# A planned kernel on one core: layer 1's activation and tails worked in PSUM, GpSimd's passes cut into 256 columns

## The chip, the core and the metric

The kernel runs on one core of a Trainium2 chip. The metric is the device time of one execution in microseconds (us), from launch to the last output; lower is better. The engines are named as in the profile: PE (TensorE's matmuls), PEld (its weight loads), DVE (VectorE), ACT (ScalarE), POOL (GpSimd) and SP (SyncE, which here only issues DMAs).

## What is computed

The first part is an attention with positive random features, for 8 batches of 8 heads, 576 positions, 64 dimensions and 128 features. The second is a two-layer network on its output, 4608 tokens of 512 features, with 2048 hidden ones; its weights come as float64.

```python
def phi(x):
    proj = einsum('bhsd,md->bhsm', x, omega)
    h = proj - sum(x * x, -1) / 2
    h = h - max(h, -1)
    return exp(h) / sqrt(m)
q_p, k_p = phi(q * scale), phi(k * scale)
num = q_p @ (k_p^T v);  den = q_p . sum(k_p) + 1e-06
x = (num / den), laid out as 4608 tokens x 512
h = x @ w_in
g = where(h > 0, h, exp(min(h, 0)) - 1)
out = g @ w_out
```

## The kernel before

The work is split twice. Attention goes by pairs of heads, 32 of them (8 batches with 4 pairs each). The network goes by 12 blocks of 384 tokens, and each block by 16 steps of 128 hidden features, 192 steps in all. The first three blocks run their steps 0 to 7 first and 8 to 15 later, so that the weights of the second half may be converted later (SPLIT, line 65).

A step has two layers. `layer1` (line 936) makes 12 matmuls into a bank of PSUM with the tag "ph", of which there are two. Numbers are kept as a high and a low part in fp32r, so each product takes three matmuls. Then ACT takes relu(-h) (L958) and exp(-that) (L959) into an SBUF tile e, DVE makes max(e - 1, h) out of e and the bank (L962), again in e. The high half g[0] is a cast of e (L967, by ACT or DVE, shown as L355 or L357 of the helper `copy`), and the low half g[1] is e minus that (L969, by POOL or DVE, shown as L360 of the helper `tt`). `layer2` (line 974) makes 9 matmuls of 512 columns into three banks acc0 to acc2, which a block keeps over its steps.

A pair is loaded (`load_pair`), its k and q are projected (`project`), k's features are summed against v (`kv`), and `finish` divides q's features by the denominator. The first 7 pairs of k and 8 of q are projected from their native layout ("native", L461), the others with fp32r parts ("tk", "tq", L512). The division has four slots of 128 columns at a time, on POOL as a rule (L706, shown as L360 hq). The first pairs, NEARLY of them, take their PSUM from the banks acc0 to acc2 and ph; later ones from three banks "pa" (`bank`, line 392).

`from_f64` (line 848) turns 512 columns of float64 weights into high and low fp32r halves: ACT L874 and L878, DVE L882, L889 and L894, POOL L897 (an integer sum, 512 columns), a cast to the high half and a subtraction for the low half on POOL (512 columns). This is done for each of the 16 slices of both weight matrices; slices of w1 are also stored in DRAM (w1s) and read again for the later blocks (w1c).

The order on each engine is not written by hand. Each operation is given to `Plan.op` with the engines that may run it, a duration in ns, a due time in us, and what it reads and writes. `Plan.order` (line 149) simulates: on each free engine the ready operation with the lowest due goes next, a bank or buffer is given in turn, and DVE operations marked `port=True` do not start in it while a POOL operation runs, nor the other way round. The result is a fixed order for each engine's queue; at run time semaphores hold it. All due times are worked out from a few numbers at the top: MLP0 is the due of the first step, SEG and STEP are the spacing of steps, LAG how far layer 2 is behind layer 1, DUE_* and *2 how far the parts of a pair lie ahead of its end, CONV* the same for the weights. ALT gives for a kind of operation by how many us the second engine is held back from taking it (negative: preferred).

```python
op("ACT", act(TB, True), due, lambda: nc.scalar.activation(e(), ph(), AF.Relu, scale=-1.0), (p,), (e,))
op("ACT", act(TB), due + 0.2, lambda: nc.scalar.activation(e(), e(), AF.Exp, scale=-1.0), (e,), (e,))
op("DVE", dve(TB), due + 0.8,
   lambda: nc.vector.scalar_tensor_tensor(e(), e(), -1.0, ph(), ALU.add, ALU.max), (p, e), (e,))
```

Of the kernel before, what the change touches and what calls it, by code (L numbers as in the profile page):

```python
# [9 lines left out]
F32 = mybir.dt.float32  # L10
# [30 lines left out]
NNAT = dict(k=7, q=8)  # L41


MLP0 = 58
SEG = [8.62, 5.76, 4.29, 5.37, 3.5, 5.86]
STEP = 4.9
STEP_ATT = 6.59

LAG = 3.08


PAIR0 = 9.46
# [12 lines left out]
SPLIT = (0, 8, 16)
NHALF = 3

DUE_Z = 12.84

NEARLY = 4  # L70

NSWAP = 8

# [198 lines left out]

ALT = dict(kv=1, out=-0.1, conv_clamp=-1, conv_hi=-1, conv_sub=2, g_hi=0, g_lo=1, y_hi=None, y_lo=-0.38, norm=2, turn=2, x_hi=0.55, sq=0.19)


def other(kind, *engs):
    return () if ALT[kind] is None else [(eng, ns, ALT[kind]) for eng, ns in zip(engs[::2], engs[1::2])]


def mm(n, m=1):

    return m * (n / 2.4 + 2.5)
# [15 lines left out]
def performer_elu_kernel(  # L300
# [58 lines left out]
    def tt(e, *args):  # L359
        (nc.vector if e == "DVE" else nc.gpsimd).tensor_tensor(*args)  # L360
# [294 lines left out]
    def finish(i, due):  # L655
# [26 lines left out]
        for g in range(3):  # L682
            d = due - 9 + g
            js = slice(4 * g, min(4 * g + 4, NJ))
            n = js.stop - js.start
            slots = [(j, j % 2, slice(0, P)) for j in range(4 * g, 4 * g + 4)]
            if g == 2:
                slots = [(8, a, slice(a * D, a * D + D)) for a in range(2)]
            hg = (h, g) if native(i, "q") else (h, min(g, 1))

            def dens(slots=slots):
                for j, a, r in slots:
                    junk = Buf(sb, [P, M], F32, "junk", f"junk_{i}_{j}_{a}", 2)
# [10 lines left out]
            op(
                "POOL", 145 + 214 * n, d + 1.2,
                lambda e, js=js, n=n: tt(  # L706
                    e, h()[:, js], h()[:, js], den()[:, js].unsqueeze(2).to_broadcast([P, n, M]), ALU.mult
                ),
                (hg, (den, g)), ((h, "n", g),), alt=other("norm", "DVE", dve(n * M)), port=True,
            )  # L710
            if i >= NTURN:
                blocks(i, g, h, qt, due - 5 + g)
                continue
            p = bank(i, "pa", f"pt_{i}_{g}")

            def turn(g=g, p=p, js=js):
                for e, j in enumerate(range(js.start, js.stop)):
                    nc.tensor.transpose(p()[:, e * P:(e + 1) * P], h()[:, j, :], ident)

            def src(g=g, p=p):  # L720
                if g == 2:
                    return p()[:, 0:P].rearrange("p (a x) -> p a x", a=2)
                return p().rearrange("p (t a x) -> p a t x", t=2, a=2)

            def dst(x, g=g):
                if g == 2:
                    return x[:, :, 512:S]
                return x[:, :, g * 256:(g + 1) * 256].rearrange("p a (t x) -> p a t x", t=2)

            d = due - 5 + g  # L730
            op("PE", 109 * n, d, turn, ((h, "n", g),), (p,))
            op(
                "ACT", act(n * P, True), d + 0.5, lambda e, src=src, dst=dst: copy(e, dst(qh()), src()), (p,), ((qh, g),),
                alt=other("turn", "DVE", dve(n * P)),
            )
# [31 lines left out]
    def blocks(i, g, h, qt, due):  # L767

        n = 4 if g < 2 else 1
        js = slice(4 * g, 4 * g + n)  # L770

        def turn():
            for o in range(2 if g == 2 else 1):
                nc.vector.transpose(
                    qt()[:, js.start + o:js.stop + o].rearrange("p j x -> p (j x)"),
                    h()[:, js].rearrange("p j x -> p (j x)"),
                )

        op("DVE", (1 if g < 2 else 2) * dve(n * P), due, turn, ((h, "n", g),), ((qt, g),))

    def output(i, qt, due):

# [65 lines left out]
    def from_f64(src, hi, lo, nm, due, key):  # L848
# [13 lines left out]
        def low():  # L862
            return words()[:, :, 0]
# [4 lines left out]
        def ui():  # L868
            return u().bitcast(I32)
# [24 lines left out]
            lambda: nc.vector.scalar_tensor_tensor(ui(), up(), -(2 ** 31), ui(), ALU.bitwise_and, ALU.bitwise_or),  # L894
            (u, (raw, 1)), (u,), port=True,
        )
        op("POOL", pool(512), due - 5, lambda: nc.gpsimd.tensor_tensor(ui(), ui(), low(), ALU.add), (u, (raw, 0)), (u,))  # L897
        op(
            "ACT", act(512), due - 4, lambda e: copy(e, hi(), u()), (u,), (key + ("h",),),
            alt=other("conv_hi", "DVE", dve(512, True)), port=True,  # L900
        )
        op(
            "POOL", pool(512), due - 3,
            lambda e: tt(e, lo(), u(), hi().bitcast(F32), ALU.subtract), (u, key + ("h",)), (key + ("l",),),
            alt=other("conv_sub", "DVE", dve(512)), port=True,
        )

    w1c, gt, acc = {}, {}, {}

    def weights(F, due):  # L910
# [4 lines left out]
        def flat():  # L915
            return t().rearrange("p a c -> p (a c)").bitcast(F32)

        both = ((t, "h"), (t, "l"))
        if blk == 0:
            from_f64(w1[f], lambda: t()[:, 0], lambda: t()[:, 1], f"w1_{f}", due, (t,))  # L920
            op("SP", 500, due, lambda: nc.sync.dma_start(w1s[f], flat()), both, (("w1s", f),), P * 4096)
# [14 lines left out]
    def layer1(F, due):  # L936
# [15 lines left out]

        for c in range(NC):
            reads = [(z, k) for k in ring(blk) if k[1] == c for z in ("xh", "xl")]
            op("PE", mm(TB, 3), due + 0.5 * c, lambda c=c: mms(c), [*reads, (w, "h"), (w, "l")], (p,))
        due += 2

        op("ACT", act(TB, True), due, lambda: nc.scalar.activation(e(), ph(), AF.Relu, scale=-1.0), (p,), (e,))  # L958
        op("ACT", act(TB), due + 0.2, lambda: nc.scalar.activation(e(), e(), AF.Exp, scale=-1.0), (e,), (e,))  # L959
        op(  # L960
            "DVE", dve(TB), due + 0.8,
            lambda: nc.vector.scalar_tensor_tensor(e(), e(), -1.0, ph(), ALU.add, ALU.max), (p, e), (e,),  # L962
        )
        first, second = ("ACT", act(TB)), ("DVE", dve(TB, True))
        if blk:
            first, second = second, first
        op(*first, due + 1.2, lambda x: copy(x, g()[:, 0], e()), (e,), ((g, 0),), alt=other("g_hi", *second), port=True)  # L967
        op(
            "POOL", pool(TB), due + 1.5,  # L969
            lambda x: tt(x, g()[:, 1], e(), g()[:, 0].bitcast(F32), ALU.subtract), (e, (g, 0)), ((g, 1),),  # L970
            alt=other("g_lo", "DVE", dve(TB)), port=True,
        )

    def layer2(F, due):
        blk, f, f0, f1 = STEPS[F]
        g = gt.pop(F)
        for tt in range(NTT):
# [157 lines left out]
```

## Time and profile before

| | us |
|---|---|
| median of 3 runs | 1058.7 (1058.46 to 1059.76) |
| the profiled execution | 1058.12 |
| its span, first to last instruction | 1056.3 |
| busy: PE, ACT, DVE, POOL | 1024.7, 725.9, 674.9, 488.1 |

The profiled execution is the one that every row below comes from. Its span leaves out 1.8 us around the instructions. Matmuls are pipelined, so two that follow each other overlap in the rows and PE's busy time is a union. The granted TensorE clock was 0.992 of full speed in the mean.

### The profile page before, as it was taken

How to read it: one execution, taken by the hardware profiler on the slowest of the kernel's cores; microseconds unless marked ns; L12 is line 12 of the kernel's file. 1: busy time of each engine (PE TensorE's matmuls, PEld its weight loads, DVE VectorE, ACT ScalarE, POOL GpSimd, SP SyncE). 2: the span in 40 equal slices, each digit the busy share in tenths (PEclk: the TensorE clock that was granted, in tenths of full speed). 3: DMA queues.
4: the chain of work that ended last, by engine and by line, in shares of the span. 5: the costliest groups of instructions: out<-in, count | busy, mean ns of one | idle time of the engine just before them, and what ended most of it. 6: DMA issues, size and time to landing. Idle time of an engine off the chain costs nothing.

```text
span 1056.3 us, 22323 instructions
## 1 busy us (share of the span) xinstructions
PE 1024.7 (97%) x7171; PEld 903.2 (86%) x7171; DVE 674.9 (64%) x2626; ACT 725.9 (69%) x2154; POOL 488.1 (46%) x504
## 2 busy tenths in 40 slices
PE   7987989999999999999999999999999999999998
PEld 6776778789988888898888888998888888899997
DVE  5899888694688877324778787424777786422222
ACT  6987875584888996328999998327999898322221
POOL 1675645565465455224465555323544664322221
PEclk8999999999999999999999999999999999999999
DMA  6655667566764755444755556434665553444431
GB/s 199 175 179 157 196 233 240 190 227 238 228 214 136 232 187 171 151 137 133 238 168 187 181 185 211 153 120 139 202 191 180 190 182 97 143 138 137 150 121 69
DMA packets 70533, 185.00 MB, mean 175 GB/s; under 512 B 7952, under 2 KB 23504, under 8 KB 70416
## 3 DMA queue, kind: packets, MB, share of 16 engines
q1 hardware_dynamic: 70416, 183.57, 53.3%
q8 instruction: 58, 0.95, 0.4%
q14 instruction: 59, 0.48, 0.1%
HBM read 161.78 MB, written 21.76 MB: 174 GB/s over the span
## 4 chain that ended last, share of the span: by engine, by line
PE 77%; ACT 1%; DMA 1%; issue 1%; DVE 0%; POOL 0%; SPq 0%; POOLq 0%; DVEq 0%
PE ph L949 11%; PE acc L983 11%; PE acc L985 11%; PE ph L951 11%; PE acc L984 11%; PE ph L950 11%; PE pn L795 3%; PE pkv L573 3%; PE ppq L512 3%; PE ppk L512 2%; DMA w1c<-w1s 1%; PE pz L672 1%; DMA xk<-in_kx_dram 0%; ACT hk L428 0%; PE pkv L583 0%
## 5 line engine op out<-in xcount | busy, mean ns | idle before, releaser
L360 POOL TENSOR_TENSOR g<-e,g 128x384 fp32r<-128x384 f32 x174 | 190.6, 1095 | 392.6 <-DVE g L357 321.4
L949 PE MATMUL ph<-xh,w1c 128*128 128x384 f32 x768 | 264.1, 344 | 3.2 <-DVE e L962 1.6
L951 PE MATMUL ph<-xh,w1c 128*128 128x384 f32 x768 | 258.9, 337 | 0.0
L950 PE MATMUL ph<-xl,w1c 128*128 128x384 f32 x768 | 258.3, 336 | 0.0
L962 DVE SCALAR_TENSOR_TENSOR e<-e,ph 128x384 f32<-128x384 f32 x192 | 105.8, 551 | 218.1 <-ACT e L959 213.0
L958 ACT ACTIVATE e<-ph 128x384 f32<-128x384 f32 x192 | 94.1, 490 | 205.7 <-PE ph L951 204.1
L983 PE MATMUL acc<-w2h,g 128*128 128x512 f32 x576 | 230.3, 400 | 0.1
L985 PE MATMUL acc<-w2h,g 128*128 128x512 f32 x576 | 228.1, 396 | 1.2 <-DVE g L360 1.1
L984 PE MATMUL acc<-w2l,g 128*128 128x512 f32 x576 | 227.9, 396 | 0.0
L949 PEld LDWEIGHTS ph<-xh,w1c 128*128 128x128 f32 x768 | 144.6, 188 | 21.4 <-issue 6.0
L950 PEld LDWEIGHTS ph<-xl,w1c 128*128 128x128 f32 x768 | 144.7, 188 | 9.8
L951 PEld LDWEIGHTS ph<-xh,w1c 128*128 128x128 f32 x768 | 144.3, 188 | 0.0
L985 PEld LDWEIGHTS acc<-w2h,g 128*128 128x128 f32 x576 | 108.3, 188 | 27.6 <-DVE g L360 2.0
L983 PEld LDWEIGHTS acc<-w2h,g 128*128 128x128 f32 x576 | 108.3, 188 | 13.9 <-issue 2.1
L984 PEld LDWEIGHTS acc<-w2l,g 128*128 128x128 f32 x576 | 108.4, 188 | 8.9
L959 ACT ACTIVATE e<-e 128x384 f32<-128x384 f32 x192 | 101.2, 527 | 3.4
L360 POOL TENSOR_TENSOR hq<-hq,den 128x512 f32<-128x512 f32 (+1 forms) x96 | 82.4, 873 | 19.7 <-DVE den L703 18.1
L694 DVE CUSTOM_DVE_ANT_0 junk<-hq,pz 128x128 f32<-128x128 f32 (+1 forms) x320 | 73.8, 280 | 9.9 <-PE pz L672 8.8
L530 DVE CUSTOM_DVE_ANT_0 hk<-ppk,p2k 128x128 f32<-128x128 f32 x225 | 56.7, 287 | 29.1 <-ACT p2k L521 27.6
L521 ACT ACTIVATE p2k<-ppk,sqk 128x128 f32<-128x128 f32 x225 | 68.1, 368 | 6.0 <-PE ppk L512 5.1
L521 ACT ACTIVATE p2q<-ppq,sqq 128x128 f32<-128x128 f32 x216 | 66.8, 366 | 7.6 <-PE ppq L512 4.6
L428 ACT ACTIVATE hk<-hk,nbk 128x128 f32<-128x128 f32 x225 | 71.4, 399 | 0.5
(105 smaller groups left out, 1641.5 us busy)
## 6 DMA issues: line engine op xcount, KB each, us to landing
w1c<-w1s SPq DMA_DIRECT2D x176, 512.0 KB, 3.4
raw_w<-in_w_dram SPq DMA_DIRECT2D x32, 512.0 KB, 4.7
xk<-in_kx_dram SPq DMA_DIRECT2D x25, 576.0 KB, 3.8
xq<-in_qx_dram SPq DMA_DIRECT2D x24, 576.0 KB, 4.7
v<-in_v_dram SPq DMA_DIRECT2D x32, 325.0 KB, 3.2
out_dram<-o SPq DMA_DIRECT2D x36, 256.0 KB, 2.5
w1s<-w1c SPq DMA_DIRECT2D x16, 512.0 KB, 4.2
zk<-kvd SPq DMA_DIRECT2D x96, 64.0 KB, 2.7
```

Of the source, the lines that this page charges most:

```text
L360: (nc.vector if e == "DVE" else nc.gpsimd).tensor_tensor(*args)
L521: nc.scalar.activation(p2()[:, a], view()[:, a, M:], AF.Identity, bias=sq()[:, j:j + 1], scale=-1.0)
L694: nc.vector.tensor_tensor_reduce(out=junk()[r], in0=h()[r, j, :], in1=pz()[r, a * P:(a + 1) * P], scale=1.0, scalar=EPS, op0=ALU.mult, op1 ...
L949: nc.tensor.matmul(ph(), wh, xh[:, c, o:o + TB], start=(c == 0), stop=False)
L950: nc.tensor.matmul(ph(), wh, xl[:, c, o:o + TB], start=False, stop=False)
L951: nc.tensor.matmul(ph(), wl, xh[:, c, o:o + TB], start=False, stop=(c == NC - 1))
L958: op("ACT", act(TB, True), due, lambda: nc.scalar.activation(e(), ph(), AF.Relu, scale=-1.0), (p,), (e,))
L959: op("ACT", act(TB), due + 0.2, lambda: nc.scalar.activation(e(), e(), AF.Exp, scale=-1.0), (e,), (e,))
L962: lambda: nc.vector.scalar_tensor_tensor(e(), e(), -1.0, ph(), ALU.add, ALU.max), (p, e), (e,),
L983: nc.tensor.matmul(a(), g()[:, 0, ts], w2h[:, f], start=(f == f0), stop=False)
L984: nc.tensor.matmul(a(), g()[:, 0, ts], w2l[:, f], start=False, stop=False)
L985: nc.tensor.matmul(a(), g()[:, 1, ts], w2h[:, f], start=False, stop=(f == f1 - 1))
```

## The change

Layer 1: L962 writes its result back into the bank ph instead of e. The cast to g[0] and the subtraction for g[1] read ph, and the subtraction is always DVE's. In `from_f64` POOL's sum and its subtraction become two instructions of 256 columns each, and in `finish` the division by the denominator becomes two instructions of two slots. What reads those results now waits for both. NEARLY goes from 4 to 6, and the numbers of due times and preferences are others.

```diff
-MLP0 = 58
-SEG = [8.62, 5.76, 4.29, 5.37, 3.5, 5.86]
-STEP = 4.9
+MLP0 = 116.09
+SEG = [7.76, 5.18, 3.52, 6.03, 3.08, 6.08]
+STEP = 5.77
-LAG = 3.08
-PAIR0 = 9.46
-DUE_LOAD, DUE_K, DUE_KV, DUE_Q = 27.64, 25.53, 12.92, 18.02
-LOAD2, K2, KV2, Q2 = 56.0, 46.17, 29.33, 32.74
-TAIL = 11.71
-TAIL2 = 4.06
+LAG = 3.07
+PAIR0 = 6.93
+DUE_LOAD, DUE_K, DUE_KV, DUE_Q = 13.33, 24.73, 12.92, 16.61
+LOAD2, K2, KV2, Q2 = 61.91, 48.81, 29.33, 33.34
+TAIL = 12.08
+TAIL2 = 3.52
-CONV1 = 13.71
-CONV_STEP = -0.51
-CONV2 = 0.84
-CONV3 = 70.47
+CONV1 = 15.65
+CONV_STEP = -0.39
+CONV2 = 0.86
+CONV3 = 64.8
-DUE_Z = 12.84
-NEARLY = 4
+DUE_Z = 12.4
+NEARLY = 6
-ALT = dict(kv=1, out=-0.1, conv_clamp=-1, conv_hi=-1, conv_sub=2, g_hi=0, g_lo=1, y_hi=None, y_lo=-0.38, norm=2, turn=2, x_hi=0.55, sq=0.19)
+ALT = dict(kv=1.9, out=-5.74, conv_clamp=1.29, conv_hi=9.8, conv_sub=2.06, g_hi=0.02, g_lo=5.17, y_hi=None, y_lo=2.7, norm=0.24, turn=1.44, x_hi=-0.5, sq=-0.57)
...
-            op(
-                "POOL", 145 + 214 * n, d + 1.2,
...
+            for x in range((n + 1) // 2):
+                jx = slice(js.start + 2 * x, min(js.start + 2 * x + 2, js.stop))
+                nx = jx.stop - jx.start
+                op(
+                    "POOL", 145 + 214 * nx, d + 1.2,
+                    lambda e, jx=jx, nx=nx: tt(
+                        e, h()[:, jx], h()[:, jx], den()[:, jx].unsqueeze(2).to_broadcast([P, nx, M]), ALU.mult
+                    ),
+                    (hg, (den, g)), ((h, "n", g, x),), alt=other("norm", "DVE", dve(nx * M)), port=True,
+                )
...
-        op("POOL", pool(512), due - 5, lambda: nc.gpsimd.tensor_tensor(ui(), ui(), low(), ALU.add), (u, (raw, 0)), (u,))
+        for x in range(2):
+            cs = slice(256 * x, 256 * x + 256)
+            op(
+                "POOL", pool(256), due - 5,
+                lambda cs=cs: nc.gpsimd.tensor_tensor(ui()[:, cs], ui()[:, cs], low()[:, cs], ALU.add),
+                (u, (raw, 0)), ((u, x),),
+            )
...
-        op(
-            "POOL", pool(512), due - 3,
-            lambda e: tt(e, lo(), u(), hi().bitcast(F32), ALU.subtract), (u, key + ("h",)), (key + ("l",),),
+        for x in range(2):
+            cs = slice(256 * x, 256 * x + 256)
+            op(
+                "POOL", pool(256), due - 3,
+                lambda e, cs=cs: tt(e, lo()[:, cs], u()[:, cs], hi()[:, cs].bitcast(F32), ALU.subtract),
+                ((u, x), key + ("h",)), (key + ("l", x),),
+                alt=other("conv_sub", "DVE", dve(256)), port=True,
+            )
...
         op(
             "DVE", dve(TB), due + 0.8,
-            lambda: nc.vector.scalar_tensor_tensor(e(), e(), -1.0, ph(), ALU.add, ALU.max), (p, e), (e,),
-        )
-        first, second = ("ACT", act(TB)), ("DVE", dve(TB, True))
+            lambda: nc.vector.scalar_tensor_tensor(ph(), e(), -1.0, ph(), ALU.add, ALU.max), (p, e), (p,),
+        )
+        first, second = ("ACT", act(TB, True)), ("DVE", dve(TB))
         if blk:
             first, second = second, first
-        op(*first, due + 1.2, lambda x: copy(x, g()[:, 0], e()), (e,), ((g, 0),), alt=other("g_hi", *second), port=True)
-        op(
-            "POOL", pool(TB), due + 1.5,
-            lambda x: tt(x, g()[:, 1], e(), g()[:, 0].bitcast(F32), ALU.subtract), (e, (g, 0)), ((g, 1),),
-            alt=other("g_lo", "DVE", dve(TB)), port=True,
+        op(*first, due + 1.2, lambda x: copy(x, g()[:, 0], ph()), (p,), ((g, 0),), alt=other("g_hi", *second))
+        op(
+            "DVE", dve(TB), due + 1.5,
+            lambda: nc.vector.tensor_tensor(g()[:, 1], ph(), g()[:, 0].bitcast(F32), ALU.subtract), (p, (g, 0)), ((g, 1),),
         )
```

## Rows read from the trace of the kernel before

**Rows 1.** The page: busy us, share, instructions of each engine.

```profile
PE 1024.7 (97%) x7171; PEld 903.2 (86%) x7171; DVE 674.9 (64%) x2626; ACT 725.9 (69%) x2154; POOL 488.1 (46%) x504
```

**Rows 2.** Busy us by stretch: PE, PEld, DVE, ACT, POOL; clock, DMA, GB/s.

```profile
0.00:25.00 25.00, 18.62 (x102) 16.75 (x102) 12.41 (x32) 14.95 (x42) 3.17 (x8) 0.80 0.65 188
...
25.00:150.00 125.00, 108.91 (x727) 89.62 (x727) 113.01 (x366) 102.97 (x311) 78.64 (x65) 0.97 0.58 182
...
150.00:250.00 100.00, 94.69 (x490) 84.14 (x489) 77.43 (x149) 62.37 (x143) 59.34 (x51) 1.00 0.67 224
...
250.00:910.00 660.00, 659.85 (x5091) 584.64 (x5089) 435.58 (x2001) 509.63 (x1585) 313.48 (x349) 1.00 0.54 177
```

**Rows 3.** Two DVE lines, whole span: ns min/median/max, first, last start.

```profile
L882 DVE TENSOR_SCALAR u_w<-u_w x31: 412/420/1526, 14.5 to 235.1; 128x512 f32<-128x512 f32 x31
...
L894 DVE SCALAR_TENSOR_TENSOR u_w<-raw_w,u_w x32: 673/686/1798, 17.0 to 238.4; 128x512 int32<-128x512 int32 x32
```

**Rows 4.** Groups on DVE, 0 to 210 us: busy us, mean ns, idle before.

```profile
L894 DVE SCALAR_TENSOR_TENSOR u_w<-raw_w,u_w 128x512 int32<-128x512 int32 x27 | 23.3, 867 | 0.3
...
L882 DVE TENSOR_SCALAR u_w<-u_w 128x512 f32<-128x512 f32 x27 | 18.4, 686 | 2.3 <-ACT u_w L874 2.2
...
L889 DVE TENSOR_SCALAR u_w<-u_w 128x512 int32<-128x512 int32 x28 | 18.2, 656 | 0.2
...
L360 DVE TENSOR_TENSOR g<-e,g 128x384 fp32r<-128x384 f32 x15 | 15.7, 1047 | 2.4 <-ACT g L355 2.4
...
L357 DVE CAST g<-e 128x384 fp32r<-128x384 f32 x7 | 2.9, 415 | 0.2
```

**Rows 5.** Groups on POOL, 0 to 210 us, same columns.

```profile
L897 POOL TENSOR_TENSOR u_w<-u_w,raw_w 128x512 int32<-128x512 int32 x27 | 40.8, 1513 | 43.4 <-DVE u_w L894 30.9 <-ACT hq L428 6.7 <-issue 5.8
...
L360 POOL TENSOR_TENSOR w2l<-u_w,w2h 128x512 fp32r<-128x512 f32 x16 | 22.6, 1412 | 24.6 <-DVE w2h L357 18.4 <-ACT w2h L355 6.1
...
L360 POOL TENSOR_TENSOR hq<-hq,den 128x512 f32<-128x512 f32 x16 | 17.0, 1071 | 6.1 <-DVE den L703 4.8 <-ACT nbk L434 1.2
...
L597 POOL TENSOR_TENSOR zs<-zs,hk 128x256 f32<-128x256 f32 x1 | 0.7, 747 | 0.1
```

**Rows 6.** Groups that read PSUM, 0 to 210 us, same columns.

```profile
L761 DVE TENSOR_TENSOR xl<-pn,xh 128x320 fp32r<-128x320 f32 x8 | 3.9, 484 | 0.1
...
L357 DVE COPY o<-acc 128x512 f32<-128x512 f32 x2 | 1.4, 692 | 0.7 <-POOL w2l L360 0.7
...
L355 ACT CAST xh<-pn 128x320 fp32r<-128x320 f32 x7 | 3.2, 463 | 0.5 <-PE pn L748 0.5
```

**Rows 7.** PE's timeline: start, us, instruction, idle before, releaser.

```profile
60.48 0.44 PE L461 MATMUL ppk<-of,xk 128*64 128x128 f32 x4 [0.64 <-ACT hk L428]
...
63.29 2.67 PE L461 MATMUL ppq<-of,xq 128*128 128x128 f32 x20 [1.15 <-ACT hk L428]
...
103.98 0.33 PE L718 MATMUL pt<-ident,hq 128*128 128x128 f32 x1 [3.79 <-ACT hq L428]
```

**Rows 8.** Timeline of all engines at 181 us, same columns.

```profile
181.25 0.54 DVE L962 SCALAR_TENSOR_TENSOR e<-e,ph 128x384 f32<-128x384 f32 x1
...
181.83 0.51 ACT L355 CAST g<-e 128x384 fp32r<-128x384 f32 x1 [2.99 <-DVE e L962]
...
181.85 0.44 PE L949 MATMUL ph<-xh,w1c 128*128 128x384 f32 x1 [1.56 <-DVE e L962]
...
182.37 0.56 DVE L360 TENSOR_TENSOR g<-e,g 128x384 fp32r<-128x384 f32 x1 [0.58 <-ACT g L355]
```

**Rows 9.** Timeline: L962 and the next matmul on its bank, two steps.

```profile
70.92 0.55 DVE L962 SCALAR_TENSOR_TENSOR e<-e,ph 128x384 f32<-128x384 f32 x1
...
72.27 0.42 PE L949 MATMUL ph<-xh,w1c 128*128 128x384 f32 x1
...
260.14 0.56 DVE L962 SCALAR_TENSOR_TENSOR e<-e,ph 128x384 f32<-128x384 f32 x1 [0.25 <-ACT e L959]
...
261.02 0.34 PE L949 MATMUL ph<-xh,w1c 128*128 128x384 f32 x1
```

More of the change, by code (lines that the diff above doesn't have):

```diff
@@ L703, in finish @@
             op("DVE", 100, d + 0.5, lambda dg=dg: nc.vector.reciprocal(dg(), dg()), ((den, g),), ((den, g),))
-            op(
-                "POOL", 145 + 214 * n, d + 1.2,
[L706 to L709, printed above, removed]
-            )
+            for x in range((n + 1) // 2):
[8 more added lines that the diff above has]
+                )
+            normed = [(h, "n", g, x) for x in range((n + 1) // 2)]
             if i >= NTURN:
@@ L730, in finish @@
             d = due - 5 + g
-            op("PE", 109 * n, d, turn, ((h, "n", g),), (p,))
+            op("PE", 109 * n, d, turn, normed, (p,))
             op(
@@ L777, in turn @@
                 )
-        op("DVE", (1 if g < 2 else 2) * dve(n * P), due, turn, ((h, "n", g),), ((qt, g),))
+        op("DVE", (1 if g < 2 else 2) * dve(n * P), due, turn, [(h, "n", g, x) for x in range(1 if g == 2 else 2)], ((qt, g),))
     def output(i, qt, due):
@@ L896, in from_f64 @@
         )
-        op("POOL", pool(512), due - 5, lambda: nc.gpsimd.tensor_tensor(ui(), ui(), low(), ALU.add), (u, (raw, 0)), (u,))
+        for x in range(2):
[5 more added lines that the diff above has]
+            )
         op(
-            "ACT", act(512), due - 4, lambda e: copy(e, hi(), u()), (u,), (key + ("h",),),
+            "ACT", act(512), due - 4, lambda e: copy(e, hi(), u()), ((u, 0), (u, 1)), (key + ("h",),),
             alt=other("conv_hi", "DVE", dve(512, True)), port=True,
         )
-        op(
-            "POOL", pool(512), due - 3,
-            lambda e: tt(e, lo(), u(), hi().bitcast(F32), ALU.subtract), (u, key + ("h",)), (key + ("l",),),
-            alt=other("conv_sub", "DVE", dve(512)), port=True,
-        )
+        for x in range(2):
[6 more added lines that the diff above has]
+            )
     w1c, gt, acc = {}, {}, {}
@@ L916, in flat @@
             return t().rearrange("p a c -> p (a c)").bitcast(F32)
-        both = ((t, "h"), (t, "l"))
+        both = ((t, "h"), (t, "l", 0), (t, "l", 1))
         if blk == 0:
@@ L954, in layer1 @@
             reads = [(z, k) for k in ring(blk) if k[1] == c for z in ("xh", "xl")]
-            op("PE", mm(TB, 3), due + 0.5 * c, lambda c=c: mms(c), [*reads, (w, "h"), (w, "l")], (p,))
+            op("PE", mm(TB, 3), due + 0.5 * c, lambda c=c: mms(c), [*reads, (w, "h"), (w, "l", 0), (w, "l", 1)], (p,))
         due += 2
@@ L987, in layer2 @@
             d = due + 0.65 * tt
-            op("PE", mm(DM, 3), d, mms, ((g, 0), (g, 1), ("w2", f, "h"), ("w2", f, "l")), (acc[tt],))
+            op("PE", mm(DM, 3), d, mms, ((g, 0), (g, 1), ("w2", f, "h"), ("w2", f, "l", 0), ("w2", f, "l", 1)), (acc[tt],))
             if f < f1 - 1:
```

## The prediction, made before the changed kernel had run

> **What bounds the kernel now.** I read the page's busy shares first: TensorE is busy 1024.7 us of the span, 97% [rows 1], so at most some 31 us can be had without removing matrix work, and the change removes none. Then the table by stage [rows 2], which says where those 31 us lie: 6.4 idle in the first 25 us, 16.1 from 25 to 150 (125.00 - 108.91), 5.3 from 150 to 250, 0.15 in the 660 us from 250 to 910, and the rest at the end. The reader is to see that the steady stage is closed: PE is never without work there, so nothing that DVE, ACT or POOL save between 250 and 910 can be worth time. The change is decided in the first 250 us. Of these, 25 to 150 is the stage with the most to gain, and there DVE is busy 113.01 of 125, more than PE (108.91), ACT (102.97) or POOL (78.64): in that stage DVE is the fullest engine, so I cost the change in DVE time first, and then look at who waits for a bank of PSUM.
>
> Two things make DVE slow there. Instructions that read two SBUF tiles or run in the fast SBUF mode are usually as short as their median (0.42 us for L882, 0.69 for L894) and sometimes 1.5 to 1.8 us [rows 3]; they are long when a POOL instruction runs. Their means up to 210 us are 686, 656 and 867 ns [rows 4]. And layer 1's lower half, where the planner gives it to DVE, takes 1047 ns in the mean there [rows 4]. Instructions with one operand in PSUM show no such spread.
>
> **The change part by part.** All sums are against the profiled run's own time, 1058.12 us, which is 0.6 below the median of 1058.7.
>
> *Tails and casts from PSUM.* 22 steps of layer 1 lie before 210 us. Before, 15 tails ran on DVE (15.7 us) and 7 on POOL; the DVE casts were 7 (2.9 us), the other 15 ran on ACT [rows 4]. After, all 22 tails are on DVE with one PSUM operand. That form is there for other tiles: 320 columns take 484 ns, and a 512-column copy from PSUM 692, so 1.08 ns a column and 553 ns for 384 [rows 6]. Tails: 22 x 0.553 = 12.2 instead of 15.7, -3.5 us. Casts from PSUM: 7 x (0.553 - 0.415) = +1.0. Together -2.5 us of DVE. If all 22 casts fell to DVE it would be 22 x 0.553 - 2.9 = +9.3 for them; I keep the split, since ACT's cast of 320 columns from PSUM takes 463 ns [rows 6] and costs no more than now. The Trainium skill (VectorE: DVE Perf Modes, "Why PSUM operands drop a tier") speaks against this part: a PSUM operand takes the fp32 copy out of its two-per-cycle mode. The trace agrees, 692 ns from PSUM against a fast 512-column instruction's 420; by a cast that kept its 415 ns the sum would be 1.0 us lower.
>
> *POOL in halves of 256 columns.* The three conversion forms lose to POOL, before 210 us, 27 x (0.686 - 0.420) = 7.2 us (L882), 28 x (0.656 - 0.420) = 6.6 (L889, same form), 27 x (0.867 - 0.686) = 4.9 (L894) [rows 3, 4]: 18.7 in all. A POOL instruction half as long holds them up half as long: -9.3. Ends: 0 if the second half always starts before DVE gets in, -18.7 if every collision goes. With the tails DVE has 11.8 us less to do. How much of that is on the path? In 25 to 150 DVE has work 90% of the time but PE's waits also end on ACT; I take half, **-6 us**, ends 0 and -11.8.
>
> The price is on POOL: 256 columns take 747 ns [rows 5], so a pair of halves 1.49 us, against 1.51 for the sums and 1.41 for the conversion tails as they are now, and 1.07 for the norms [rows 5]. For conversions that is under 0.1 us each and hidden: POOL is idle 46 us between 25 and 150. If that cover were gone, 25 tails x 0.1 = 2.5 us. For the norms it is +0.4 for each 512-column group; only the last pair before the first layer 1 has nothing behind it: **+0.4**, upper end 0.4 x 8 pairs = 3.2.
>
> *NEARLY 4 to 6.* Pairs 4 and 5 project into the acc banks, which layer 2 needs only later, and leave the three pa banks to the turns. PE waited for ACT to free a projection's bank at 60.48 (0.64), 63.29 (1.15) and 103.98 (3.79) [rows 7]. The first two are of pairs 4 and 5 and go; the third is a turn behind pair 6's projection, whose maximum is late in DVE's queue; I give it a third: **-3.0 us**, ends 0 and -5.6. The pkv and pz of pairs 4 and 5 now take ph banks; that cost is in the next term.
>
> *The ph bank is held longer.* Before, ph was free after L962. Now L962 writes into ph, and cast and tail read it. There are two banks, PE alternates, and PE's queue is in order: a layer 1 that waits holds every matmul behind it. The step at 181 us shows what is added: L962 ends at 181.79, cast and tail end at 182.93, 1.14 later, and PE had already waited 1.56 us for that L962 [rows 8]. Of the first 34 steps, up to 262 us, 11 had less than 1.14 us between L962's end and the first matmul on the same bank, from 0.80 at 72.27 to 0.32 at 261.02 [rows 9]. At 0.6 us missing in each, that is 6.8 us if PE's order stayed; the order is planned anew with the longer hold and layer 2 can fill in, so I take **+2.5**, ends 0 and +6.8.
>
> *Orders and preferences.* MLP0 moves every due alike and costs nothing. Loads of the first pairs rank 14 us later in SP's queue, and behind the weights' transfers; hidden by two buffers, and if that cover is gone the price is of the size of the 1.15 us waits above, a few at most. In the steady stage DVE gains 128 x 0.553 = 71 us of tails and loses many two-tile subtractions to POOL; 435.58 + 71 of 660 [rows 2] leaves it below PE: **0**. What ends last there is still PE.
>
> Sum: -6 + 0.4 - 3.0 + 2.5 = -6.1, so 1052.0 on the profiled run and 1052.6 on the median; I say **1052.5**.
>
> **Rivals.** *The ph bank paces the start (slower).* For it: eleven thin margins, and a wait of PE on L962 already there [rows 8, 9]. Against it: cast and tail no longer wait for POOL's 1.1 us or lose the port. It decides when cast plus tail end over 1.1 us behind L962 with no layer 2 ready. All 6.8 us are lost, DVE's relief ends in waiting, only the 1.8 us of pairs 4 and 5 stay: about 1063.7. *All of DVE's relief is on the path.* -11.8 - 5.6 + 2.5: about 1044. For it: DVE is the fullest engine; against it: ACT has 103 of 125. *Nothing much: the halving does not shorten the waits* because POOL puts its halves back to back, and PE's idle time belongs to ACT and to the chain of one pair. Then -1.2 (half of the tails) - 1.8 + 2.5 + 0.4 = -0.1, and 1058.6. That is the case in which the change does not do what it says.
>
> **How the numbers follow.** The forecast with its own range (1047 to 1056.5) has 0.47, the large gain 0.14, no change 0.15, the ph bank 0.24. The range reaches from -17 (DVE and banks at their lower ends) to +5 (the ph rival): 1042 to 1064. About 0.2%, 2.1 us, is what a measurement of this kernel tells from no change. Faster 0.61, same 0.15, slower 0.24.
>
> **What would show it.** Right: PE idle in 25 to 150 falls from 16 to about 9 us; the means of L882 and L889 come down toward 0.55 us and their longest from 1.5 to about 1.2; layer 1's tail is one DVE form of 0.53 to 0.57 us with no long ones; the wait at 104 us shrinks; 250 to 910 stays without PE idle time. Wrong: waits of the first layer 1 matmul on the DVE tail appear between 130 and 260 us (the ph rival); or L882 and L889 keep their means (the halves are back to back); or PE shows idle time behind 250 us, where I have put none.

## The result and the profile after

The changed kernel takes 1043.13 us in the median (1038.98 to 1043.66, 4 runs), the one before 1058.58 beside it: 15.5 us less. The ratio of the means is 0.9844 (95% interval 0.9817 to 0.987), 16.5 us; where a difference below is called one by the ratio, it is worked out so. The profiled execution took 1043.66 us and its span is 1041.9. So the sign was right, and the size was not: 6.1 us were forecast. The time stands where the second rival put it (about 1044), but that is luck: its sum was 11.8 us of DVE and 5.6 of banks less 2.5, and the experiments below divide the gain otherwise.

Busy time of the changed kernel, as in [rows 1], then its stages as in [rows 2] (PE, PEld, DVE, ACT, POOL; clock, DMA, GB/s):

```profile
PE 1026.1 (98%) x7171; PEld 906.3 (87%) x7171; DVE 683.0 (66%) x2758; ACT 738.8 (71%) x2119; POOL 421.7 (40%) x535
```

```profile
0.00:25.00 25.00, 20.56 (x118) 18.24 (x119) 14.41 (x43) 16.18 (x49) 4.36 (x11) 1.00 0.76 198
25.00:150.00 125.00, 118.69 (x767) 101.08 (x767) 108.22 (x355) 106.77 (x307) 90.46 (x120) 0.96 0.65 207
150.00:250.00 100.00, 99.65 (x526) 89.57 (x526) 67.53 (x167) 71.16 (x173) 59.28 (x73) 1.00 0.66 224
250.00:900.00 650.00, 649.00 (x5078) 573.18 (x5077) 450.53 (x2122) 496.79 (x1499) 267.56 (x333) 1.00 0.55 175
```

PE does the same work (1026.1 us busy, 1024.7 before) in a shorter span. Its idle time fell from 6.4 to 4.4 us in the first stage, from 16.1 to 6.3 in the second and from 5.3 to 0.35 in the third; between 250 and 900 us it rose from 0.15 to 1.0. That is the whole gain, and it lies where the prediction looked, except the third stage, where I had put a loss. The 2 us of the first stage are not shown to be the change's: in a second profile of the changed kernel (after_again, the last experiment) the four stages have 6.2, 7.3, 0.7 and 0.5 us of idle time.

The groups of DVE up to 210 us that answer to [rows 4], with count, busy us, mean ns and the idle time ahead of them. L886, L893 and L898 are the conversion lines L882, L889 and L894 of before; L983 is the tail and L357 the cast of layer 1:

```profile
L898 DVE SCALAR_TENSOR_TENSOR u_w<-raw_w,u_w 128x512 int32<-128x512 int32 x30 | 24.2, 807 | 0.2
L886 DVE TENSOR_SCALAR u_w<-u_w 128x512 f32<-128x512 f32 x31 | 19.0, 617 | 3.6 <-ACT u_w L878 3.6
L893 DVE TENSOR_SCALAR u_w<-u_w 128x512 int32<-128x512 int32 x31 | 18.1, 587 | 0.3
...
L983 DVE TENSOR_TENSOR g<-ph,g 128x384 fp32r<-128x384 f32 x27 | 15.0, 554 | 1.5 <-ACT g L355 1.2
...
L357 DVE CAST g<-ph 128x384 fp32r<-128x384 f32 x13 | 7.2, 555 | 0.7
```

The tail takes 554 ns in the mean where it took 1047, and none of the 192 was longer than 560 ns. The three conversion lines came down by 60 to 70 ns each, not by half of what they lost to POOL. Nor did the longest of L893 come down as forecast: 1532 ns, behind a subtraction of 576 columns on POOL (tk, 1.49 us at 136.62) that the change does not cut. On POOL, the groups that answer to [rows 5]:

```profile
L905 POOL TENSOR_TENSOR u_w<-u_w,raw_w 128x256 int32<-128x256 int32 x60 | 47.6, 812 | 45.1 <-DVE u_w L898 27.7 <-issue 10.1 <-ACT w2h L355 3.3
L360 POOL TENSOR_TENSOR w2l<-u_w,w2h 128x256 fp32r<-128x256 f32 x32 | 25.3, 817 | 6.0 <-ACT w2h L355 5.9
...
L360 POOL TENSOR_TENSOR hq<-hq,den 128x256 f32<-128x256 f32 x31 | 19.7, 658 | 7.6 <-ACT hq L428 3.7 <-DVE den L703 3.2 <-ACT raw_w L882 0.4
```

And who PE waited for, the longest, over the whole span (us, times, longest):

```profile
PE pn L752 <- ACT qh L355: 2.6, 2, 2.2
...
PE ph L962 <- DVE g L983: 0.3, 1, 0.3
```

Once, by 0.3 us, a layer 1 had to wait for the tail that now holds its bank (0.7 us in all in the second profile).

### The profile page after: what moved, and what is told of

Same layout as the page of the kernel before. It is cut to its first block, busy times and chain, and to the rows that moved or that the text cites. A ratio compares the mean times of both kernels' runs of the same rounds, so it can differ in the third digit from the quotient of the medians.

```text
span 1041.9 us, 22241 instructions
## 1 busy us (share of the span) xinstructions
PE 1026.1 (98%) x7171; PEld 906.3 (87%) x7171; DVE 683.0 (66%) x2758; ACT 738.8 (71%) x2119; POOL 421.7 (40%) x535
## 4 chain that ended last, share of the span: by engine, by line
PE 87%; ACT 4%; DMA 4%; DVE 2%; issue 1%; POOL 1%; SPq 0%; DVEq 0%; POOLq 0%; ACTq 0%
PE ph L962 12%; PE acc L995 12%; PE acc L997 12%; PE acc L996 12%; PE ph L964 12%; PE ph L963 12%; PE pn L799 3%; PE pkv L573 3%; PE ppq L512 3%; PE ppk L512 3%; DMA xq<-in_q_dram 2%; DMA xk<-in_kx_dram 1%; ACT hk L428 1%; PE ppq L461 1%; PE pkv L631 1%
## 5 line engine op out<-in xcount | busy, mean ns | idle before, releaser
L962 PE MATMUL ph<-xh,w1c 128*128 128x384 f32 x768 | 263.6, 343 | 0.5 <-DVE g L983 0.3
L975 DVE SCALAR_TENSOR_TENSOR ph<-e,ph 128x384 f32<-128x384 f32 x192 | 107.5, 560 | 179.2 <-ACT e L972 178.5
L971 ACT ACTIVATE e<-ph 128x384 f32<-128x384 f32 x192 | 94.6, 493 | 155.2 <-PE ph L964 154.3
L962 PEld LDWEIGHTS ph<-xh,w1c 128*128 128x128 f32 x768 | 144.7, 188 | 19.7 <-DVE g L983 3.0
L360 POOL TENSOR_TENSOR tk<-xk,tk 64x576 fp32r<-64x576 f32 x44 | 63.0, 1431 | 226.9 <-ACT tk L355 222.6
L983 DVE TENSOR_TENSOR g<-ph,g 128x384 fp32r<-128x384 f32 x192 | 106.1, 552 | 36.3 <-ACT g L355 34.3
L360 POOL TENSOR_TENSOR hq<-hq,den 128x256 f32<-128x256 f32 (+1 forms) x158 | 89.1, 593 | 71.5 <-DVE den L703 65.4
L355 ACT CAST g<-ph 128x384 fp32r<-128x384 f32 x129 | 62.3, 483 | 52.8 <-DVE ph L975 52.0
L360 POOL TENSOR_TENSOR tq<-xq,tq 64x576 fp32r<-64x576 f32 x48 | 68.4, 1425 | 76.0 <-ACT tq L355 43.3
```

What stands on the lines that cost most here:

```text
L962: nc.tensor.matmul(ph(), wh, xh[:, c, o:o + TB], start=(c == 0), stop=False)
L975: lambda: nc.vector.scalar_tensor_tensor(ph(), e(), -1.0, ph(), ALU.add, ALU.max), (p, e), (p,),
L983: lambda: nc.vector.tensor_tensor(g()[:, 1], ph(), g()[:, 0].bitcast(F32), ALU.subtract), (p, (g, 0)), ((g, 1),),
```

## The experiments

Two ways of asking were used, and the difference between them turned out to matter. Some kernels were planned anew with one part changed, so that their whole order moved. Others kept the planned order instruction for instruction and only changed what an instruction does: there nothing but the part in question differs.

### Code and numbers apart, planned anew

**The code of before, the numbers of after.**

```diff
-MLP0 = 58
+MLP0 = 116.09
...
-ALT = dict(kv=1, out=-0.1, conv_clamp=-1, ...
+ALT = dict(kv=1.9, out=-5.74, conv_clamp=1.29, ...
```

> The code of before with the due times, preferences and NEARLY of after. Theory A (the new order takes the gain): 1044 to 1051 us, PE idle between 25 and 150 us down from 16.1 to under 9. Theory B (the shorter and uncontended instructions on DVE take it): 1055 to 1062 us, PE idle there still over 14. In between, 1051 to 1055: both, and the two parts add.

1049.96 us, ratio 0.992 (0.9892 to 0.9948): 8.5 us by the ratio, PE idle 7.4 us from 25 to 150.

**The code of after, the numbers of before** (the diff above, the other way round, in the changed kernel).

> The code of after with the due times, preferences and NEARLY of before. Theory A: 1055 to 1066 us, above before where the bank ph is held longer in an order not made for it. Theory B: 1044 to 1051 us. If the two parts add, this one's gain and the gain of the numbers alone sum to 15.5 us.

1056.66 us, ratio 0.9988 (0.9974 to 1.0003). 1.3 us and 8.5 us do not add up to 16.5 (all by ratios). The stages of the code alone (columns as above) show something else:

```profile
25.00:150.00 125.00, 111.20 (x740) 91.79 (x741) 105.38 (x357) 109.57 (x320) 87.95 (x112) 0.97 0.62 194
150.00:250.00 100.00, 99.44 (x503) 89.12 (x502) 65.61 (x144) 58.67 (x129) 54.31 (x68) 1.00 0.64 218
250.00:900.00 650.00, 645.21 (x5010) 570.45 (x5009) 466.41 (x2042) 530.44 (x1647) 183.80 (x273) 1.00 0.53 176
```

The first 250 us got better (13.8 and 0.6 us idle against 16.1 and 5.3), and 4.8 us of idle time appeared between 250 and 900, where before had 0.1. I took the preferences for the cause, since DVE had 466 of 650 us there.

### The order of after kept, the instructions put back

**POOL's halves joined again**, at the place of the second half:

```diff
-lambda cs=cs: nc.gpsimd.tensor_tensor(ui()[:, cs], ui()[:, cs], low()[:, cs], ALU.add)
+lambda x=x: x and nc.gpsimd.tensor_tensor(ui(), ui(), low(), ALU.add)
...
-lambda e, cs=cs: tt(e, lo()[:, cs], u()[:, cs], hi()[:, cs].bitcast(F32), ALU.subtract)
+lambda e, x=x: x and tt(e, lo(), u(), hi().bitcast(F32), ALU.subtract)
```

(the norms alike)

> The order of after, instruction for instruction, but POOL's two halves (sum, subtraction, norms) are one instruction again, put where the second half stands. Theory B says that DVE's waits for POOL come back: L886 and L893 from 0.60 to about 0.67 us in the mean, 31 instructions each and 30 of L898, some 6 us of DVE's time, 2 to 6 us of the run: 1045 to 1049. Theory A: within 2 us of after, 1041 to 1045.

1044.94 us, ratio 0.9866 (0.9832 to 0.99): 2.3 us over after by the ratios, inside both intervals. DVE's groups up to 210 us:

```profile
L898 DVE SCALAR_TENSOR_TENSOR u_w<-raw_w,u_w 128x512 int32<-128x512 int32 x30 | 24.5, 816 | 0.2
L893 DVE TENSOR_SCALAR u_w<-u_w 128x512 int32<-128x512 int32 x30 | 21.5, 718 | 0.3
L886 DVE TENSOR_SCALAR u_w<-u_w 128x512 f32<-128x512 f32 x30 | 17.4, 584 | 2.2 <-ACT u_w L878 2.2
...
L983 DVE TENSOR_TENSOR g<-ph,g 128x384 fp32r<-128x384 f32 x26 | 14.4, 553 | 1.3 <-ACT g L355 1.0
```

L893 loses 131 ns each, L886 gains 33, L898 loses 9: 21.5 + 17.4 + 24.5 us against 18.1 + 19.0 + 24.2, though after has one L893 and one L886 more by 210 us. Over all 32 slices the durations sum to 66.6 us here and 64.0 in after, so halving relieves DVE's conversion of 2 to 3 us in this order, not of 9.

**Layer 1's activation in SBUF again:**

```diff
-lambda: nc.vector.scalar_tensor_tensor(ph(), e(), -1.0, ph(), ALU.add, ALU.max), (p, e), (p,),
+lambda: nc.vector.scalar_tensor_tensor(e(), e(), -1.0, ph(), ALU.add, ALU.max), (p, e), (p,),
...
-lambda x: copy(x, g()[:, 0], ph())
+lambda x: copy(x, g()[:, 0], e())
...
-nc.vector.tensor_tensor(g()[:, 1], ph(), g()[:, 0].bitcast(F32), ALU.subtract)
+nc.vector.tensor_tensor(g()[:, 1], e(), g()[:, 0].bitcast(F32), ALU.subtract)
```

> The order of after, instruction for instruction, but layer 1's activation goes into its SBUF tile again, and cast and subtraction read that. The bank ph is free after the activation, as before. Theory B: the subtraction meets POOL again, its mean goes from 554 ns to 800 or more up to 210 us, 27 of them, some 7 us of DVE's time: 1045 to 1050. The rival from the prediction (holding the bank costs time): under 1041, for the bank is let go over 1 us earlier. Theory A: 1041 to 1045.

1048.23 us, ratio 0.9901 (0.9872 to 0.993): 6.0 us slower than after by the ratios. The bank is free earlier and the kernel is slower all the same, so what PSUM saves is worth more than what the bank costs in this order. (The tail now holds the tile e in place of the bank, and there are two of e; ACT's L971 shows no wait for it here, and one of 1.1 us in the next run.) The tail and the cast up to 210 us:

```profile
L983 DVE TENSOR_TENSOR g<-e,g 128x384 fp32r<-128x384 f32 x27 | 20.9, 774 | 1.9 <-ACT g L355 1.6
...
L357 DVE CAST g<-e 128x384 fp32r<-128x384 f32 x13 | 8.3, 639 | 0.6
```

**Both put back.** The two diffs above together.

> The order of after with POOL's instructions whole and layer 1's activation in SBUF: both instruction changes undone, only the order is new. If the two add, 1043.1 + 1.8 + 5.1, so 1048 to 1052; if whole POOL instructions make the collisions of the SBUF tail longer (up to 1.1 us each instead of 0.5), 1052 to 1057.

1053.75 us, ratio 0.9967 (0.9953 to 0.9981). Its stages and its groups on DVE up to 210 us:

```profile
25.00:150.00 125.00, 116.65 (x761) 98.09 (x761) 117.75 (x351) 107.60 (x306) 81.42 (x68) 0.99 0.63 207
150.00:250.00 100.00, 97.33 (x504) 87.36 (x503) 73.77 (x155) 66.55 (x157) 54.99 (x44) 0.98 0.63 212
250.00:900.00 650.00, 646.88 (x5003) 569.97 (x5003) 466.66 (x2114) 499.81 (x1504) 275.18 (x285) 1.00 0.54 175
```

```profile
L898 DVE SCALAR_TENSOR_TENSOR u_w<-raw_w,u_w 128x512 int32<-128x512 int32 x30 | 26.3, 876 | 0.2
L983 DVE TENSOR_TENSOR g<-e,g 128x384 fp32r<-128x384 f32 x26 | 23.3, 896 | 1.2 <-ACT g L355 0.9
L893 DVE TENSOR_SCALAR u_w<-u_w 128x512 int32<-128x512 int32 x30 | 20.8, 696 | 0.3
L886 DVE TENSOR_SCALAR u_w<-u_w 128x512 f32<-128x512 f32 x30 | 18.7, 628 | 2.7 <-ACT u_w L878 2.7
...
L357 DVE CAST g<-e 128x384 fp32r<-128x384 f32 x13 | 11.5, 882 | 0.6
```

This is a square of four kernels with one order. Ratio to before:

| | POOL whole | POOL in halves |
|---|---|---|
| activation in SBUF | 0.9967 | 0.9901 |
| activation in PSUM | 0.9866 | 0.9844 |

The order with the old instructions gains 3.5 us, the instructions 13.0 more. In the medians of this square each part alone is worth more than what it adds to the other: halves 7.0 us without PSUM and 2.3 with it, PSUM 10.7 without halves and 6.0 with them. The 2.3 lies inside the intervals, and the 4.7 us between the two rows of the square are no more than what the four intervals together leave open (some 5 us), so the times alone do not show that the parts overlap. The durations do: a tail or a cast on SBUF waits until a POOL instruction has ended (896 and 882 ns), with halves it waits less (774 and 639), from PSUM it does not wait at all (554 and 555). Up to 210 us these five groups take 100.6 us of DVE with both put back and 83.5 in after: 17.1 us of relief, 12.6 of them in tail and cast.

That it is POOL they wait for can be read instruction by instruction. Of the five groups I call one held up when it took over 30 ns more than its short duration (420 ns for L886 and L893, 685 for L898, 555 for a tail, 357 for a cast on SBUF). Up to 210 us:

| kernel | conversion: held up, mean wait, total | tails and casts: held up, mean wait, total |
|---|---|---|
| before | 25 of 82, 0.75 us, 18.7 us | 9 of 22, 0.87 us, 7.8 us |
| before, POOL in halves (next run) | 38 of 83, 0.39, 14.9 | 13 of 22, 0.43, 5.6 |
| after's order, both put back | 28 of 90, 0.73, 20.3 | 21 of 39, 0.75, 15.8 |
| after's order, SBUF, halves | 38 of 91, 0.42, 16.1 | 26 of 40, 0.37, 9.6 |
| after's order, PSUM, POOL whole | 26 of 90, 0.69, 17.9 | from PSUM: none |
| after | 40 of 92, 0.37, 14.9 | from PSUM: none |

In these six kernels all 264 waits end with a POOL instruction: the instruction's end less its short duration lies 127 to 143 ns before that POOL instruction's end, every time, and no wait goes through more than one POOL instruction. Halves cut a wait to about half, but there are 1.2 to 1.5 times as many. Of after's 27 tails, 19 ran beside a POOL instruction, and they took 553 ns in the mean against 555 for the others.

**POOL in halves in the order of before:**

```diff
-lambda: nc.gpsimd.tensor_tensor(ui(), ui(), low(), ALU.add)
+lambda: [nc.gpsimd.tensor_tensor(ui()[:, c], ui()[:, c], low()[:, c], ALU.add) for c in (slice(0, 256), slice(256, 512))]
```

(the subtractions and norms alike)

> The order of before, with each of POOL's sums, subtractions and norms sent as two instructions one behind the other. In the order of after, with layer 1 in SBUF, halves were worth 1053.75 - 1048.2 = 5.5 us. If the halving does that by itself, 1050 to 1055; if POOL gets its second half in before DVE (the prediction's case without a gain): 1057 to 1060.

1053.79 us, ratio 0.9961 (0.9948 to 0.9975): 4.1 us faster than before with no other change. DVE does get in between two halves that stand one behind the other: none of its 51 waits up to 210 us outlasted more than one POOL instruction. Its groups on DVE up to 210 us, against [rows 4] (L883 and L890 are L882 and L889 there):

```profile
L890 DVE TENSOR_SCALAR u_w<-u_w 128x512 int32<-128x512 int32 x28 | 18.2, 655 | 0.2
L883 DVE TENSOR_SCALAR u_w<-u_w 128x512 f32<-128x512 f32 x27 | 14.9, 557 | 3.6 <-ACT u_w L875 3.4
...
L360 DVE TENSOR_TENSOR g<-e,g 128x384 fp32r<-128x384 f32 x15 | 12.5, 836 | 1.7 <-ACT g L355 1.7
```

One of the two conversion lines fell from 686 to 557 ns, the other did not move (656 and 655), and the tail, of which I had not thought in this term, fell from 1047 to 836.

### Single numbers, planned anew, and how much an order is worth

**The preferences of before in after** (`ALT` of before), **the due times of before in after** (MLP0 to DUE_Z of before), **NEARLY at 4:**

```diff
-NEARLY = 6
+NEARLY = 4
```

> After with the preferences between engines (ALT) of before; code, due times and NEARLY are those of after. In the code alone PE was idle 4.8 us between 250 and 900 us, where DVE had 466 of 650 us; theory C says that the preferences give this back (fp32r subtractions of k and q go to POOL): PE idle there 3 to 6 us and 1047 to 1053 us in all. If the due times do it, no idle time comes back there: 1042 to 1046.

> After with the due times of before; code, preferences and NEARLY are those of after. If the preferences and NEARLY with the code make the gain: 1043 to 1047 us. If the due times do: 1050 to 1057, with PE idle between 25 and 150 us back over 12.

> After with NEARLY at 4 again, all else as after. The prediction's term of 3 us for the banks of pairs 4 and 5: 1045 to 1048, with PE waits for the exponentials of pairs 4 and 5 between 55 and 110 us. If the banks do not matter in the new order: 1042 to 1044.5.

1049.96 us (ratio 0.9939, 0.9922 to 0.9957), 1051.55 (0.995, 0.9927 to 0.9973) and 1050.25 (0.994, 0.9922 to 0.9957). Each alone takes 10 us or more from after by the ratio, and all three together can't be worth that: the sum is over 30 us, and with all three (the code alone) 15.2 are lost. The due times of before left 11.5 us of idle time in 25 to 150, between its two forecasts, and its ten runs lie 10 us apart (1046.41 to 1056.46). Theory C, that the preferences cause the idle time behind 250 us, fell: with the preferences of before PE is idle 0.5 us between 250 and 900, not 3 to 6. With NEARLY at 4 the stage 25 to 150 has 14.4 us of idle time, with the prediction's slower rival among it: a layer 1 that waits for the tail to leave its bank (PE in order of time: start, duration, in brackets the wait):

```profile
71.09 0.69 PE L962 MATMUL ph<-xh,w1c 128*128 128x384 f32 x1 [2.98 <-DVE g L983]
```

**Neighbours of an order.** So I moved one due time by so little that only the order can matter.

```diff
-DUE_LOAD, DUE_K, DUE_KV, DUE_Q = 13.33, 24.73, 12.92, 16.61
+DUE_LOAD, DUE_K, DUE_KV, DUE_Q = 13.33, 24.73, 12.92, 16.71
```

> After with one due time moved by 0.1 us (DUE_Q 16.61 to 16.71), which changes the planned order but nothing else. Theory D (the numbers are tuned to this kernel, and any other order costs some us): 1046 to 1053 us, so that what NEARLY or the preferences seemed to be worth when planned anew is in good part the loss of a tuned order. Rival: orders so close are alike, 1042 to 1045.

> After with DUE_K 24.73 to 24.83, as the run beside it: theory D 1046 to 1053 us, its rival 1042 to 1045.

> Before with DUE_K 25.53 to 25.93, which changes its planned order. If before was tuned as closely as after: 1061 to 1067 us. If before's order was nothing special: 1055 to 1060.

After: 1046.09 us (ratio 0.9879, 0.9862 to 0.9895) with DUE_Q at 16.71, 1049.16 (0.9913, 0.9886 to 0.9941) with DUE_K at 24.83. Before with DUE_K at 25.93: 1055.55 (0.9964, 0.995 to 0.9978), faster than before itself. A tenth of a microsecond in a due time moved the changed kernel by 3.7 us (its interval just touches after's) and 7.3.

**The same for the two halves of the change** (DUE_K and DUE_Q of the code alone by 0.4 and 0.5, DUE_K of the numbers alone by 0.1):

> The code of after with the numbers of before, but DUE_K 25.53 to 25.93: another planned order of the same code. If the code alone had an unlucky order: 1046 to 1053 us, near before's gain from halves alone (1053.8) or better. If the code is worth nothing without its numbers: 1055 to 1060.

> As the run beside it with DUE_Q 18.02 to 18.52: 1046 to 1053 if the order of the code alone was unlucky, 1055 to 1060 if the code is worth nothing without its numbers.

> The code of before with the numbers of after, DUE_K 24.73 to 24.83. If the gain of the numbers (8.5 us) belongs to one order: 1054 to 1059. If it belongs to the numbers: 1047 to 1052.

Code: 1050.14 us (0.9924, 0.9905 to 0.9943) and 1058.87 (1.0004, 0.9989 to 1.0019). Numbers: 1060.63 (1.002, 1.0003 to 1.0037). So the 8.5 us of the numbers alone belonged to one order: a neighbour lost them all, 10.6 us away. The code alone lies between 0 and 8.0 us in three orders. A part that is judged by planning anew is judged with an error of some 5 to 10 us, and the runs with NEARLY, ALT and the due times say no more than that after's order is a good one.

### Two attempts to do better

**Norms whole again in the order of after** (the conversion stays in halves).

> The order of after with the norms of q_p whole again and the conversion in halves. The norms run on to 907 us, the conversion ends at 240. If the conversion's halves carry the gain of the halving: within 1.5 us of after or under it, for whole norms are some 0.2 us shorter each. If the norms' halves matter: 1044.5 to 1047.

1043.73 us, ratio 0.9858 (0.9823 to 0.9893), the same as after within the intervals: the norms' halves neither cost nor gain anything that shows.

**The conversion in quarters**, beside the changed kernel itself:

```diff
-lambda cs=cs: nc.gpsimd.tensor_tensor(ui()[:, cs], ui()[:, cs], low()[:, cs], ALU.add)
+lambda x=x: [nc.gpsimd.tensor_tensor(ui()[:, c], ui()[:, c], low()[:, c], ALU.add)
+             for c in (slice(256 * x, 256 * x + 128), slice(256 * x + 128, 256 * x + 256))]
```

(the subtraction alike)

> The order of after, with each half of POOL's conversion (256 columns) sent as two instructions of 128 columns, one behind the other. If what is left of the collisions goes down by half again: some 6 us less on DVE before 210 us and 2 to 4 us less in all, about 1040. If the fixed part of a POOL instruction (some 0.1 us, 128 more of them) or the re-entry of POOL before DVE takes it back: 1042 to 1046.

> The changed kernel unaltered, beside the quarters on the same chip: 1041 to 1045 us, ratio to before 0.982 to 0.987.

1045.76 us, ratio 0.9879 (0.986 to 0.9898), against 1042.31, 0.9844 (0.9822 to 0.9866) for after on the same chip: slower by 3.5 us in the medians, with intervals that overlap by 0.0006. POOL's conversion sums of the quarters by source line (shortest, median and longest ns, first and last start):

```profile
L905 POOL TENSOR_TENSOR u_w<-u_w,raw_w x128: 447/464/974, 17.7 to 220.9; 128x128 int32<-128x128 int32 x128
```

And two of its groups on DVE up to 210 us, against those of after:

```profile
L886 DVE TENSOR_SCALAR u_w<-u_w 128x512 f32<-128x512 f32 x30 | 21.7, 729 | 4.7 <-ACT u_w L878 4.3 <-POOL u_w L905 0.5
L893 DVE TENSOR_SCALAR u_w<-u_w 128x512 int32<-128x512 int32 x30 | 15.7, 526 | 0.3
```

L893 gained 61 ns and L886 lost 112, but most of that loss is one instruction: the L886 at 117.95 took 3.25 us, held through six POOL instructions one behind the other, and without it the mean is 642. The three conversion lines together take 61.8 us of DVE up to 210 us against after's 61.3 (with two more instructions there), so quarters bring DVE next to nothing. A quarter costs POOL 464 ns in the median, so four cost 1.86 us where two halves cost 1.50 (2 x 749). DVE meets shorter instructions and more of them (51 waits of 0.32 us in the mean, where after has 40 of 0.37). Why that one L886 did not get in between six is open. No version here beats the changed kernel.

## Why the prediction was right in sign and wrong in size

- **The stages.** Right: idle time of PE in the first 250 us was what there was to gain, and 25 to 150 fell from 16.1 to 6.3, under the 9 I named. From 250 on the loss was 0.9 us where I had put 0. But "the steady stage is closed" is not a law: with both instruction changes put back it had 3.1 us of idle time, in the code alone 4.8.
- **The tails.** This is the step that failed. The unit price was right: 553 ns were forecast for either, 554 were measured for the tail and 555 for the cast. The comparison was not. I set the new tails against the mix of before, where 15 tails were DVE's and 7 POOL's, and took a cast on SBUF at 415 ns, as if it would go on meeting POOL so seldom; that gave 2.5 us of DVE, of which I took half. In the order of after DVE has 26 or 27 tails and 13 casts by 210 us. On SBUF with POOL whole they cost 34.8 us, on SBUF with halves 29.2 (20.9 + 8.3), from PSUM 21.6 with POOL whole (14.4 + 7.2) and 22.2 with halves, one tail more. So PSUM spares 13.2 us of DVE where POOL is whole and 7.0 where it is in halves, and by the ratio it is worth 10.7 and 6.0 us of time.
- **The halves.** -9.3 us of DVE were forecast for the conversion. With the order kept, the three lines fell by 2.6 us over all slices in after's order and by 4.2 in before's. "Half as long" was right for a single wait (0.75 to 0.39 us in before's order, 0.69 to 0.37 in after's); what I left out is that twice as many instructions are met more often (25 waits against 38, 26 against 40). Where the tails are on SBUF, half the length pays for them too, 5.6 us (34.8 to 29.2), a term I did not have. DVE does get in between: the case without a gain did not come.
- **Half on the path.** DVE's relief was 17.1 us and not 11.8, and the two kernels that it lies between are 13.0 us apart by ratio. The two numbers have different bases: 17.1 is against after's order with the old instructions, where DVE is busy 117.75 of the 125 us; against the kernel before, DVE fell from 113.01 to 108.22 there. And not all of the 13.0 comes from those 210 us: 2.1 us of PE's idle time between 250 and 900 went as well (3.1 to 1.0). In the two profiled runs, which lie 8.2 us apart, the first 250 us account for 6.1 us of PE's idle time. So what share of DVE's relief reached the end stays open, between these 6.1 and 10.9 (13.0 less 2.1) of 17.1. Whether ACT's 103 of 125 us, the reason I gave for only half, held the rest back is not shown; but for the one at the start, PE's four longest waits after the change all end on ACT (2.6, 2.2, 1.7 and 1.3 us).
- **The bank.** +2.5 forecast, upper end 6.8 (eleven times 0.6 is 6.6); measured in after a single wait of 0.3 us (0.7 in the second profile, 1.4 in three waits with POOL whole). The planner had made room: from the end of L975 to the next matmul on its bank no step of the first 40 has less than 1.29 us, where in before 11 of 34 had less than 1.14. Counted from the tail's end, 21 of the 40 have less than 1.14 us left. The row I took as its sign, PE's 1.56 us for L962 at 181.85 [rows 8], was DVE's trouble with POOL. In front of that L962 stood two of the long ones (DVE and POOL of the kernel before in order of time: start, duration):

```profile
177.81 1.41 POOL L360 TENSOR_TENSOR w2l<-u_w,w2h 128x512 fp32r<-128x512 f32 x1 [2.35 <-DVE w2h L357]
177.98 1.65 DVE L360 TENSOR_TENSOR g<-e,g 128x384 fp32r<-128x384 f32 x1
...
179.17 1.60 POOL L897 TENSOR_TENSOR u_w<-u_w,raw_w 128x512 int32<-128x512 int32 x1
...
179.55 1.78 DVE L894 SCALAR_TENSOR_TENSOR u_w<-raw_w,u_w 128x512 int32<-128x512 int32 x1
```

  The tail ends 0.41 us behind the first POOL instruction, L894 0.56 behind the second, each its own short duration less some 0.13 us. An uncollided pair of them takes 0.56 + 0.69 us; 2.2 us of the delay were POOL's, and they went with the change. So did the 5.3 us of idle time between 150 and 250, where I had put a loss. Elsewhere the rival is real: 2.98 us in one wait with NEARLY at 4.
- **NEARLY.** -3.0 forecast; 10 us were lost without it, but neighbours of the order lose 3.7 and 7.3 for nothing. The term is neither borne out nor refuted.
- **Orders at nothing.** The largest gap in the working. I priced the new due times by single covers and put MLP0 and the rest at 0. Orders that differ by a tenth of a microsecond in one due time stand up to 10.6 us apart, more than the whole forecast.

With the sizes as measured the sum reads: the order with the old instructions -3.5, the instruction forms -13.0, together -16.5 by ratio. The forecast had -3.0 for the first (the banks of pairs 4 and 5, with 0 for the rest) and -3.1 for the second (-6, +0.4, +2.5). So the miss of 10 us lies in the instruction forms, the tails and casts above all; that the order's number fits is luck, with neighbours so far apart. What remains open is how much of after's order could be had with the old instructions if it were searched for; and the bank's price by itself, since no kernel here reads PSUM and lets the bank go early.

## What to carry to other kernels

Before pricing an instruction by its mean, look at its shortest and its longest: where the median is 0.42 us and the longest 1.5, the mean holds waits, and the question is which operands make it wait and which form would not. Cutting the instruction that is waited for shortens each wait but makes more of them; a form that does not wait ends them. When a late instruction seems to be the cause of a wait, read what stood in front of it in its queue. And where an order is planned by a program, measure two or three neighbours of it before crediting a part with its difference, or keep the order and change the instruction alone.

## What the runs showed of the hardware

A DVE instruction with two SBUF operands, and L886, L893 and a cast with their one operand in SBUF, waited where a POOL instruction was under way, and went on 127 to 143 ns before that one's recorded end (264 waits in six kernels, the table above); with one operand in PSUM it did not wait (none of after's 192 tails over 560 ns).

POOL's time for an int32 sum of two SBUF tiles is a fixed part and a slope. The conversion's sums by source line, as for the quarters above, in the kernel before:

```profile
L897 POOL TENSOR_TENSOR u_w<-u_w,raw_w x32: 1276/1479/1855, 17.9 to 241.0; 128x512 int32<-128x512 int32 x32
```

and in the changed one:

```profile
L905 POOL TENSOR_TENSOR u_w<-u_w,raw_w x64: 732/749/1254, 18.1 to 217.1; 128x256 int32<-128x256 int32 x64
```

The shortest take 1276 ns for 512 columns, 732 for 256 and, in quarters, 447 for 128. That is 2.1 to 2.2 ns a column and some 0.16 to 0.19 us for each instruction, which I had put at under 0.1 by comparing means that held waits.

Runs of one kernel differ by several us: after from 1038.98 to 1044.31 in two series, before from 1056.38 to 1064.07 in its widest. In the profiled run of after the granted clock fell to half, 1.2 GHz, at 109.6 us, for 10.2 us. By then PE had waited 2.22 us, worked 1.2, and stood in a second wait, of 0.47 (PE in order of time: start, duration, what ran, and in brackets what it waited for before):

```profile
108.33 1.19 PE L752 MATMUL pn<-qh,kvf 128*64 128x256 f32 x8 [2.22 <-ACT qh L355]
109.99 2.08 PE L461 MATMUL ppq<-of,xq 128*128 128x128 f32 x8 [0.47 <-ACT hq L428]
...
112.30 3.51 PE L631 MATMUL pkv<-v,hk 128*128 128x65 f32 x16
```

The sixteen matmuls at 112.30 took 3.51 us there; in the repeated run, at the full clock, the same sixteen took 1.90. That run had nearly the same two waits (1.84 and 0.46 us, at 109.00 and 112.03), and the clock did not fall: the stage 25 to 150 was granted 1.00 throughout. In the first 25 us it was the other way about, 0.80 there and 1.00 here. Its span was 1040.5, 1.4 us less; whether that is the clock's doing was not tried, nor what made the clock fall.
